# A fused attention-and-mixer kernel: the order of TensorE written out as a table of steps

## The chip, the cores and the metric

One core of a Trainium2 chip runs the program. The metric is the device time of one execution in microseconds (us); the kernel before was timed three times, and one further execution was recorded by the hardware profiler. Engine names are those of the profile: PE is TensorE (PEld its weight loads), DVE is VectorE, ACT is ScalarE, POOL is GpSimd, SP is SyncE, which here only issues DMAs. A name with a q (POOLq, SPq) is an engine's queue of issued DMAs.

## The reference

There are 8 batches with 8 heads, 512 tokens of 64 values each, and a state of 32 rows per head. Tokens read from the state, the state reads from the tokens, and the 544 rows that come out are mixed per batch.

```python
# attention, x: [8, 8, 512, 64], state: [8, 8, 32, 64]
scores = scale * x @ state.T           # softmax over the 32 state rows
xread  = softmax(scores) @ state
scores2 = scale * state @ x.T          # softmax over the 512 tokens
sread  = softmax(scores2) @ x
x = concat([xread, sread])             # [8, 544, 512] with the heads joined
# mixer, w_q and w_k: [512, 64], w_out: [512, 512]
wq, wk = x @ w_q, x @ w_k
W_tok  = scale2 * wq @ wk.T            # [544, 544] per batch
out    = relu(W_tok @ x) @ w_out       # [8, 544, 512]
```

Neither kernel builds `xread` or `W_tok`. Both use that the products are associative: `wq` is taken as (softmax) times (state times `w_q`), and `W_tok @ x` as `wq` times (`wk.T @ x`).

## The kernel before, in words

All of x, 8 MiB in float32, is brought in at the start. Batch 0 arrives as float32 in four pieces (`x_f0`, L71, issued from ACT) and is cast to bf16 by DVE and ACT (L427, L429). The other seven batches (`x_bf1` to `x_bf7`, L88 and L90) and `w_out` (L92, between batches 2 and 3) are cast by their DMA, which POOL issues. The state (`st_f`, L69 and L72) and `w_q`, `w_k` (`w_f`, L76) come through SP.

One batch goes through these steps, each with a matmul group on PE and, for most, an instruction on DVE, ACT or POOL that takes the result out of PSUM:

- `s_xT`: 16 transposes of x (L147), two copies by DVE (L152).
- `s_pt`: 16 matmuls for the scores (L161), Exp by ACT into `E` (L169), a sum per row and its reciprocal by DVE (L174, L176), the normalised `A` by POOL (L178).
- `s_stbd`: POOL spreads the state into a block diagonal, two instructions (L190).
- `s_at`: 8 transposes of `A` (L203), one copy (`AT`, L207).
- `s_srd`: 32 matmuls for the state's read and 8 for its sums (L216, L226), then `srn` by DVE (L235, L237) and the block diagonal `sbd` by POOL (L242). `s_srT`: one transpose of `srn` (L253), one copy (L255).
- `s_wqk`: 4 and 8 matmuls for `wq` (L264, L273), 8 and 16 for `wk` (L285, L294), one copy each (L281 ACT, L302 DVE). `s_g` (L310, L318) and `s_v` (L326, L330, L338) make `V`, the product of `wk` and the rows.
- `s_mix` (L348): two groups of four matmuls, each with a Relu, one on ACT (L357) and one on DVE (L359); `s_mix_s` (L367, L374) is the same for the 32 state rows, kept in `rmix_s`.
- `s_fin_mm`: 16 matmuls with `w_out` (L382), two copies by ACT (L393), each followed by a DMA of 512 KB to HBM from SP (L397). The last batch is copied and stored by quarters (L403, L406). After every fourth batch `s_fin_s` does the state rows of four batches together (L412, L420).

The loop runs over ten rounds. Round i starts batch X = i (`s_xT`, `s_pt`, `s_srd`), takes batch Y = i − 1 through `s_at` to `s_v`, and finishes batch Z = i − 2. The program is written with a tile framework: the program text gives dependencies and a priority, and a list scheduler places the instructions of all five engines at compile time, each engine then running its own in that fixed order. Tiles of a pool share a number of buffers, and an instruction that writes a tile waits until the buffer's former reader is done. PSUM has eight banks: pool `psA` holds three tiles of two banks (xT, scores, mix, fin, and sw of the start), pool `psB` two tiles of one bank (all the others).

At the start `setup_st` transposes the state (L103) and copies it into `stT` (L111, L113), and `setup_sw` multiplies it with the two weights (L124, copies L135, L137).

## Time and profile before

| what | value |
|---|---|
| device time, median of 3 runs | 116.53 us (115.98 to 117.35) |
| the profiled execution's own time | 116.32 us |
| its span, first to last instruction | 114.5 us |
| PE busy | 87.3 us, 76% |
| PE weight loads busy | 54.8 us, 48% |
| DVE busy | 58.2 us, 51% |
| ACT busy | 47.3 us, 41% |
| POOL busy | 43.3 us, 38% |
| HBM read, written | 10.22 MB, 8.91 MB |

The page gives busy times for the whole span, and slices of 2.86 us below them. The busy time of PE is modelled for overlapping matmuls, so the distance from one start to the next is the better measure of what a group of matmuls costs. The page's row of the granted TensorE clock rests on records that begin only some 26 us into the span. In the timeline a row begins with its start and its duration in us; in brackets stands how long the engine had been idle, and what ended that.

### The profile page before, as it was taken

The numbers are of one execution on the slowest core, as the hardware profiler recorded it, in microseconds if no ns is written. First come the engines' busy times: TensorE is split into PE (matmuls) and PEld (weight loads), VectorE is DVE, ScalarE is ACT, GpSimd is POOL, SyncE is SP. The second block draws the span as 40 slices with busy tenths as digits, with TensorE's granted clock in tenths as the row PEclk, the third lists the DMA queues.
The fourth block names the chain that finished last, engine by engine and source line by source line (L and its number), as shares of the span: only waits on it lengthen the run. The fifth ranks groups of instructions, "written<-read, shape, count | busy, mean of one in ns | idle before, by whom it ended". The sixth has DMA issues, their size and how long they took to land. (4 is left out here: it accounts for less than half of the span.)

```text
span 114.5 us, 3055 instructions
## 1 busy us (share of the span) xinstructions
PE 87.3 (76%) x1321; PEld 54.8 (48%) x1336; DVE 58.2 (51%) x117; ACT 47.3 (41%) x70; POOL 43.3 (38%) x55
## 2 busy tenths in 40 slices
PE   0223398684979999999999989989998997949600
PEld 0002375684655657366555726565674554524200
DVE  1325565658423727852953694296449435344200
ACT  0522449030163346438442644544573454480210
POOL 8995000583990390086058107700630640000000
PEclk9999999999755999999999999999999999999995
DMA  1999999999900044040404404052332224044381
GB/s 39 290 287 183 197 204 197 199 197 198 126 0 0 6 183 182 7 186 6 183 0 189 180 3 167 24 192 77 157 154 74 104 84 183 0 203 187 87 298 48
DMA packets 14933, 15.13 MB, mean 132 GB/s; under 512 B 3656, under 2 KB 12360, under 8 KB 14920
## 3 DMA queue, kind: packets, MB, share of 16 engines
q0 software_dynamic: 7808, 4.19, 26.3%
q1 hardware_dynamic: 5736, 9.18, 22.5%
q10 hardware_dynamic: 1376, 1.57, 4.6%
q8 instruction: 10, 0.16, 0.6%
q14 instruction: 3, 0.02, 0.1%
HBM read 10.22 MB, written 8.91 MB: 167 GB/s over the span
## 5 line engine op out<-in xcount | busy, mean ns | idle before, releaser
L382 PE MATMUL fin_ps<-w_o,rmix 128*128 128x512 bf16 x113 | 32.7, 386 | 4.9 <-ACT rmix L357 2.2
L178 POOL TENSOR_TENSOR A<-E,rinv 128x1024 bf16<-128x1024 bf16 x8 | 15.3, 1912 | 47.3 <-DVE rinv L176 28.8
L393 ACT COPY ost<-fin_ps 128x1024 f32<-128x1024 f32 x14 | 14.2, 1012 | 10.8 <-PE fin_ps L382 10.4
L147 PE MATMUL xT_ps<-ident,x_bf 128*128 128x128 bf16 x128 | 13.0, 252 | 6.1 <-ACT x_bf L429 3.0
L382 PEld LDWEIGHTS <-rmix 128*128 128x128 bf16 x128 | 10.7, 99 | 14.4 <-issue 2.8
L152 DVE COPY xT<-xT_ps 128x1024 bf16<-128x1024 bf16 x16 | 11.0, 686 | 12.4 <-PE xT_ps L147 12.4
L147 PEld LDWEIGHTS <-x_bf 128*128 128x128 bf16 x128 | 9.7, 112 | 9.3 <-ACT x_bf L429 3.5
L169 ACT ACTIVATE E<-pt_ps 128x1024 bf16<-128x1024 f32 x8 | 8.2, 1023 | 11.9 <-PE pt_ps L161 11.9
L359 DVE TENSOR_SCALAR rmix<-mix_ps 128x1024 bf16<-128x1024 f32 x8 | 9.7, 1218 | 6.5 <-PE mix_ps L348 6.5
L174 DVE TENSOR_REDUCE rsum<-E 128x32 f32<-128x1024 bf16 x8 | 9.7, 1213 | 2.8 <-ACT E L169 2.8
L338 ACT ACTIVATE V<-v_ps 128x512 bf16<-128x512 f32 x8 | 4.8, 597 | 14.9 <-PE v_ps L330 14.9
L242 POOL TENSOR_TENSOR sbd<-srn,mask 128x256 bf16<-128x256 bf16 x16 | 9.5, 612 | 1.8 <-DVE srn L237 1.7
L190 POOL TENSOR_TENSOR stbd<-st_bf,mask 128x256 bf16<-128x256 bf16 x16 | 9.4, 611 | 0.0
L357 ACT ACTIVATE rmix<-mix_ps 128x1024 bf16<-128x1024 f32 x8 | 8.2, 1028 | 1.3 <-PE mix_ps L348 1.3
L103 PE MATMUL stT_ps<-ident,st_bf 128*128 128x128 bf16 x16 | 2.6, 305 | 6.9 <-DVE st_bf L96 4.0
L302 DVE CAST wk<-wk_ps 128x384 bf16<-128x384 f32 x8 | 4.4, 548 | 6.6 <-PE wk_ps L294 6.6
L348 PE MATMUL mix_ps<-wq,V 64*128 64x256 bf16 x64 | 6.7, 291 | 1.2 <-ACT V L338 0.7
L161 PE MATMUL pt_ps<-stT,xT 128*128 128x64 bf16 x128 | 6.9, 212 | 0.0
L203 PE MATMUL at_ps<-ident,A 128*128 128x128 bf16 x64 | 6.5, 244 | 0.0
L161 PEld LDWEIGHTS <-xT 128*128 128x128 bf16 x128 | 6.2, 112 | 0.4
L281 ACT CAST wq<-wq_ps 128x288 bf16<-128x288 f32 x8 | 3.2, 402 | 6.5 <-PE wq_ps L273 6.5
L90 POOL DMA_DIRECT2D x_bf<-in_x_dram x6 | 5.6, 958 | 0.0
(64 smaller groups left out, 110.1 us busy)
## 6 DMA issues: line engine op xcount, KB each, us to landing
out_dram<-ost SPq DMA_DIRECT2D x14, 512.0 KB, 2.6
x_bf<-in_x_dram POOLq DMA_DIRECT2D x7, 512.0 KB, 17.6
x_f<-in_x_dram ACTq DMA_DIRECT2D x4, 256.0 KB, 5.8
w_o<-in_moe_w_out_dram POOLq DMA_DIRECT2D x1, 512.0 KB, 13.0
out_dram<-ost_s SPq DMA_DIRECT2D x2, 256.0 KB
out_dram<-ost SPq DMA_DIRECT2D x2, 256.0 KB, 3.6
out_dram<-ost ACTq DMA_DIRECT2D x2, 256.0 KB, 4.9
st_f<-in_state_dram SPq DMA_DIRECT2D x1, 448.0 KB
```

The lines of the kernel that those rows point to most:

```text
L147: nc.tensor.transpose(out=ps[:, u, h, :], in_=x_bf[b][:, h, 128 * u : 128 * u + 128], identity=ident,)
L152: nc.vector.tensor_copy(out=xT[:, u], in_=ps[:, u])
L161: nc.tensor.matmul(out=ps[:, 2 * u : 2 * u + 2, r, NS * q : NS * q + NS], lhsT=L["xT"][:, u, h, :], rhs=stT[:, b, h, :, :], start=(h == 0) ...
L169: nc.scalar.activation(out=E.rearrange("p c r q n -> p c r (q n)"), in_=ps, func=AF.Exp, scale=float(scale))
L174: nc.vector.reduce_sum(out=rsum, in_=Ev, axis=AX.X)
L178: nc.gpsimd.tensor_tensor(out=A.rearrange("p c r q n -> p (c r q) n"), in0=Ev, in1=rinv[:, :, None].to_broadcast((128, NC * 2 * NP, NS)), ...
L190: nc.gpsimd.tensor_tensor(out=stbd[:, r], in0=st_bf[:, b, r, 0:1, :].to_broadcast((128, NP, D)), in1=mask[:, :, None].to_broadcast((128, N ...
L242: nc.gpsimd.tensor_tensor(out=sbd[:, r], in0=srn[:, r : r + 1, :].to_broadcast((128, NP, D)), in1=mask[:, :, None].to_broadcast((128, NP, D)),
L357: nc.scalar.activation(out=dst, in_=ps, func=AF.Relu)
L359: nc.vector.tensor_scalar(out=dst, in0=ps, scalar1=0.0, scalar2=None, op0=ALU.max)
L382: nc.tensor.matmul(out=L["fin"][:, c % 2, :], lhsT=rmix[:, b, k, c // 2, 128 * (c % 2) : 128 * (c % 2) + 128], rhs=w_o[:, k, :], start=(k ...
L393: nc.scalar.copy(out=L["ost"], in_=L["fin"])
```

## The change: what it does

All steps are rewritten as small functions, one for each matmul group and one for each instruction that empties it, and a table `ORDER` lists them in the order in which they are recorded. An entry is step, batch and engine: `xT1.5.t` is the second half of the transposes of batch 5 on PE, `xTe1.5.a` its copy, on ACT. `manual_schedule` for PE alone keeps PE's instructions in the order of the table; those of DVE, ACT, POOL and SP are still placed by the list scheduler, with the table's order as priority. In the table the batches run 0, 1, 2, 3, then 5, 6, 4 and 7 overlapped, and an entry ends in `1` where a matmul group of the last batch writes a one-bank tile.

What else is different:

- PSUM: `psA` holds two tiles of two banks (mix, fin, sw), `psB` four tiles of one bank. xT and the scores are split into halves of one bank, and with them the Exp (16 of 512 elements a row instead of 8 of 1024) and the row sums. Work tiles have four buffers instead of three.
- Which engine empties a tile is chosen entry by entry: ten of the 16 copies of xT, three of the 8 of `AT`, five of the 8 of `wk` go to ACT, six of the 14 copies of `ost` to DVE; of the 16 Relus over `mix` 12 are on ACT.
- Loads: of the four pieces of `x_f0` two are issued from SP, ahead of the rest of the state, and two from ACT. POOL casts one of them (`xc0`) before it issues any load of x, and casts `w_f` (`wc`) between the issues of batches 3 and 4. The issue of batch 7 stands behind the first `sbd`.
- The block diagonal of the state, `stbd`, is no longer made by POOL for each batch. POOL clears a tile for all batches, and four DMAs from SP copy `st_bf` into its diagonal blocks.
- The state's transposes are 32 of 64 columns instead of 16 of 128. The matmuls of L294 become 8 per batch instead of 16, since `srT` is stored twice side by side. Over the whole program PE has 48 matmuls and 48 weight loads less.

On POOL, the start of the program before (x_bf_74 to x_bf_80 are batches 1 to 7, stT the state's transpose) reads:

```order
masks.py:197 MEMSET ident 128x128
L79 MEMSET stT 128x1792
masks.py:199 ISA
masks.py:199 AFFINE_SELECT ident<-ident 128x128
L88 DMA x_bf_74<-in_x_dram 128x8x256
L90 DMA x_bf_75<-in_x_dram 128x8x256
L92 DMA w_o<-in_moe_w_out_dram 128x4x512
L90 DMA x_bf_76<-in_x_dram 128x8x256
L90 DMA x_bf_77<-in_x_dram 128x8x256
L90 DMA x_bf_78<-in_x_dram 128x8x256
L90 DMA x_bf_79<-in_x_dram 128x8x256
L90 DMA x_bf_80<-in_x_dram 128x8x256
```

The same engine from its clearing of `stbd` on, after the change (x_bf_69 is batch 0, x_bf_70 to x_bf_76 are batches 1 to 7, x_f_77 the float32 tile of batch 0):

```order
L124 MEMSET stbd 128x2048
masks.py:199 ISA
masks.py:199 AFFINE_SELECT ident<-ident 128x128
L152 CAST x_bf_69<-x_f_77 128x512
L146 DMA x_bf_70<-in_x_dram 128x8x256
L146 DMA x_bf_71<-in_x_dram 128x8x256
L143 DMA w_o<-in_moe_w_out_dram 128x4x512
L146 DMA x_bf_72<-in_x_dram 128x8x256
L157 CAST w_qk<-w_f 128x4x128
L158 CAST w_qk<-w_f 128x4x64
L146 DMA x_bf_73<-in_x_dram 128x8x256
L146 DMA x_bf_74<-in_x_dram 128x8x256
```

Every load of x now stands behind a cast that waits for a piece of batch 0, and those of batch 4 and later behind casts that wait for the weights.

On ACT, one full round of the program before, in the middle of the run:

```order
L169 ACTIVATE E<-pt_ps 128x1024
L393 COPY ost<-fin_ps 128x1024
L281 CAST wq<-wq_ps 128x288
L338 ACTIVATE V<-v_ps 128x512
L393 COPY ost<-fin_ps 128x1024
L357 ACTIVATE rmix<-mix_ps 128x2x2x256
L374 ACTIVATE rmix_s<-mixs_ps 128x4x32
```

And ACT after the change, from the second Relu pair on (xT_919 and xT_912 are halves of batches 6 and 5, AT, ost and G as before):

```order
L137 ACTIVATE rmix<-mix_ps 128x2x2x256 x2
L131 COPY xT_919<-xT_ps 128x1024
L131 CAST wk<-wk_ps 128x384
L131 COPY xT_912<-xT_ps 128x1024
L457 ACTIVATE V<-v_ps 128x512
L253 ACTIVATE E<-pt_ps 128x512
L137 ACTIVATE rmix_s<-mixs_ps 128x4x32
L137 ACTIVATE rmix<-mix_ps 128x2x2x256 x2
L131 COPY ost<-fin_ps 128x1024
L131 COPY srT<-srT_ps 128x256
```

The regular round is gone: copies of xT and of `wk` and both Relus of a batch now stand between the Exps on ACT.

The diff, cut to its core:

```diff
+ORDER = """
+stc.0.v stt.0.t xc0.0.p ste.0.v stf.0.a xc1.0.a ix1.0.p xc2.0.v ix2.0.p xc3.0.v xT0.0.t iwo.0.p
...
+rinv.2.v pt0.3.t srTe.2.a xT1.5.t wke.0.v exp0.3.a A.2.p xT1.4.t swe.3.v g.0.t xTe1.5.a srd.3.t
...
+    ctx.enter_context(tc.manual_schedule(engines={mybir.EngineType.PE}))
...
-    work = ctx.enter_context(tc.tile_pool(name="work", bufs=3))
-    ostp = ctx.enter_context(tc.tile_pool(name="ostp", bufs=3))
-    psA = ctx.enter_context(tc.tile_pool(name="psA", bufs=3, space=bass.MemoryType.PSUM))
-    psB = ctx.enter_context(tc.tile_pool(name="psB", bufs=2, space=bass.MemoryType.PSUM))
+    work = ctx.enter_context(tc.tile_pool(name="work", bufs=4))
+    psA = ctx.enter_context(tc.tile_pool(name="psA", bufs=2, space=bass.MemoryType.PSUM))
+    psB = ctx.enter_context(tc.tile_pool(name="psB", bufs=4, space=bass.MemoryType.PSUM))
...
-        nc.scalar.dma_start(out=x_f0[:, 2 * g : 2 * g + 2], in_=xsrc(0, 2 * g, 2 * g + 2))
+        eng = nc.sync if g % 2 == 0 else nc.scalar
+        eng.dma_start(out=x_f0[:, 2 * g : 2 * g + 2], in_=xsrc(0, 2 * g, 2 * g + 2))
...
-    nc.gpsimd.memset(stT[:, 1:B].bitcast(FP), 0.0)
-    nc.vector.memset(stT[:, 0].bitcast(FP), 0.0)
+    nc.vector.memset(stT.bitcast(FP), 0.0)
+    nc.gpsimd.memset(stbd.bitcast(FP), 0.0)
...
+    def load_x(n, b, e):
+        if n == "iwo":
+            nc.gpsimd.dma_start(out=w_o, in_=moe_w_out.rearrange("(k p) e -> p k e", p=128))
+        else:
+            b = int(n[2:])
+            nc.gpsimd.dma_start(out=x_bf[b], in_=xsrc(b, 0, H))
...
+    def w_cast(n, b, e):
+        nc.gpsimd.tensor_copy(out=w_qk[:, :, 0:2, :], in_=w_f)
+        nc.gpsimd.tensor_copy(out=w_qk[:, :, 2, :], in_=w_f[:, :, 1, :])
...
+    def st_cast(n, g, e):
+        b0, b1 = (0, 1) if g == 0 else (1, B)
+        copy(e, st_bf[:, b0:b1], st_f[:, b0:b1])
+        if g == 1:
+            for q in range(NP):
+                rows = slice(NS * q, NS * q + NS)
+                nc.sync.dma_start(
+                    out=stbd[rows, :, :, q, :].rearrange("p b r d -> p (b r) d"),
+                    in_=st_bf[rows].rearrange("p b r d -> p (b r) d"),
+                )
...
+    def xT_mm(n, b, e):
+        u = int(n[-1])
+        ps = psB.tile([128, H, 128], BF, name="xT_ps", tag="psB")
...
+    def xT_ev(n, b, e):
+        u = int(n[-1])
+        xT = work.tile([128, H, 128], BF, name=f"xT{u}")
+        copy(e, xT, L[b][f"xT{u}"])
...
+    def pt_mm(n, b, e):
+        u = int(n[-1])
+        ps = psB.tile([128, 2, 2, HN], FP, name="pt_ps", tag="psB")
...
+    def wks_mm(n, b, e):
+        ps = psB.tile([128, NC + 2, DH], FP, name="wk_ps", tag="psB")
+        for q in range(NP):
+            for h in range(2):
+                nc.tensor.matmul(
+                    out=ps[64 * h : 64 * h + 64, NC : NC + 2, :],
+                    lhsT=L[b]["srT"][:, q, :, :],
...
+    def fin_mm(n, b, e):
+        c = int(n[-1])
+        if e == "1":
+            ps = psB.tile([128, DM], FP, name="fin1_ps", tag="psB")
+            L[b][n] = ps
...
+    for tok in ORDER.split():
+        n, b, e = tok.split(".")
+        STEP[n.rstrip("0123456789")](n, int(b), e)
```

## The prediction

> **What bounds the kernel now.** I read the page first, then its table by stretches, then PE's timeline in a late round, and last the loads. Of the page:

> ```profile
> PE 87.3 (76%) x1321; PEld 54.8 (48%) x1336; DVE 58.2 (51%) x117; ACT 47.3 (41%) x70; POOL 43.3 (38%) x55
> ...
> PEclk9999999999755999999999999999999999999995
> DMA  1999999999900044040404404052332224044381
> ```

> No engine is full over the span, and the 16 DMA engines are full until slice 11, some 31 us. So I cut the span at the ends of rounds; the columns after the stretch are busy us and instructions of PE, PEld, DVE, ACT, POOL, then granted clock, DMA share, GB/s.

> ```profile
> 0.00:14.00 14.00, 2.97 (x20) 1.75 (x21) 5.25 (x19) 3.99 (x7) 9.59 (x15) 1.00 1.06 199
> 14.00:27.00 13.00, 11.12 (x192) 9.12 (x190) 8.38 (x17) 5.15 (x10) 4.19 (x5) 1.00 1.41 199
> 27.00:42.28 15.28, 12.98 (x225) 8.27 (x227) 7.43 (x17) 5.22 (x8) 9.77 (x13) 0.78 0.40 73
> ...
> 52.37:62.54 10.17, 9.54 (x155) 5.78 (x156) 6.04 (x11) 5.04 (x8) 4.23 (x6) 1.00 0.27 106
> ...
> 40.00:90.00 50.00, 47.25 (x725) 28.86 (x736) 30.20 (x55) 25.56 (x36) 19.59 (x24) 1.00 0.29 113
> ```

> From 40 us on PE is the bound: 47.25 of 50 busy, ACT 25.56 (0.51), DVE 30.20 (0.60). Before that it is not, and what it does there it does slowly:

> ```profile
> 13.81 1.06 PE L147 MATMUL xT_ps<-ident,x_bf 128*128 128x128 bf16 x8
> ...
> 28.22 0.41 PE L264 MATMUL wq_ps<-AT,sw 128*64 128x256 bf16 x4 [1.50 <-DVE AT L207]
> ...
> 33.55 1.04 PE L203 MATMUL at_ps<-ident,A 128*128 128x128 bf16 x8
> ```

> Eight transposes take 1.06 us here and 0.61 in the late round below. The page's clock of 9 in the first slices has no record behind it; by these durations PE ran at half clock at 14 us, and again at 33.5, where the page has its 7 and 5. One round of the steady part:

> ```profile
> 52.37 0.61 PE L147 MATMUL xT_ps<-ident,x_bf 128*128 128x128 bf16 x8
> 52.91 0.39 PE L348 MATMUL mix_ps<-wq,V 64*128 64x256 bf16 x4
> ...
> 53.32 0.23 PE L203 MATMUL at_ps<-ident,A 128*128 128x128 bf16 x1
> 53.68 0.29 PE L348 MATMUL mix_ps<-wq,V 64*128 64x256 bf16 x2
> ...
> 55.06 0.65 PE L161 MATMUL pt_ps<-stT,xT 128*128 128x64 bf16 x16
> 55.55 0.38 PE L382 MATMUL fin_ps<-w_o,rmix 128*128 128x512 bf16 x1
> 55.98 0.22 PE L253 MATMUL srT_ps<-ident,srn 128*128 128x128 bf16 x1
> 56.43 0.82 PE L382 MATMUL fin_ps<-w_o,rmix 128*128 128x512 bf16 x3 [0.23 <-DVE rmix L359]
> 57.18 0.41 PE L264 MATMUL wq_ps<-AT,sw 128*64 128x256 bf16 x4
> 57.52 1.25 PE L382 MATMUL fin_ps<-w_o,rmix 128*128 128x512 bf16 x5
> 58.71 0.30 PE L273 MATMUL wq_ps<-srT,w_qk 128*64 128x32 bf16 x8
> 58.94 0.41 PE L285 MATMUL wk_ps<-sw,AT 128*128 128x64 bf16 x8
> 59.28 0.41 PE L294 MATMUL wk_ps<-w_qk,srT 128*32 128x128 bf16 x16
> 59.79 0.42 PE L216 MATMUL srd_ps<-x_bf,E 128*32 128x64 bf16 x32
> 60.15 0.35 PE L226 MATMUL srd_ps<-ones,E 128*128 128x1 bf16 x8
> 60.36 0.39 PE L310 MATMUL g_ps<-wk,A 128*128 128x64 bf16 x8
> 60.81 0.38 PE L382 MATMUL fin_ps<-w_o,rmix 128*128 128x512 bf16 x1
> 61.25 0.38 PE L326 MATMUL v_ps<-sbd,wk 128*128 128x512 bf16 x1
> ...
> 61.90 0.81 PE L382 MATMUL fin_ps<-w_o,rmix 128*128 128x512 bf16 x3
> 62.54 0.22 PE L147 MATMUL xT_ps<-ident,x_bf 128*128 128x128 bf16 x1
> ```

> Read from start to start: three matmuls of L382 take 62.54 − 61.90 = 0.64, 0.21 each. A single one at 55.55 takes 0.43, so 0.22 is lost, and 0.23 more at 60.81. The one transpose at 55.98 takes 0.45 where a transpose costs 0.54/8 = 0.07: 0.38 lost. At 53.32 it is 0.36 − 0.07, at 60.36 0.45 against 0.21 for as many matmuls at 60.15, at 59.28 0.51 against 0.34 at 58.94. Together 0.22 + 0.23 + 0.38 + 0.29 + 0.24 + 0.17 = 1.5. A round of 10.17 us thus holds about 8.7 us of matmuls, and waits are 17% on top of the work.

> **What the work is.** Eight batches of 8.7 are 69.6. The state rows at the end of four batches are two groups of four L382-like matmuls, 8 × 0.21 = 1.7. The state's 32 transposes at up to 0.07 and 64 small products with the weights at up to 0.03 (eight of L273 take 0.23) are at most 4.2; I take 2.6, and as they come early little hangs on it. That is 73.9 us at full clock, against 108.7 at which the last matmul ends. The 35 us between are idle at the start, half clock and waits. The change takes hold of this, not of the work: half the matmuls of L294 would save at most 0.17 a batch, but those left load twice as many columns, and 0.34 may stay 0.34. I take 0.05 a batch, 0.4 in all: 73.5.

> **The start.** How early PE can be kept full depends on the loads.

> ```profile
> L90 POOL DMA_DIRECT2D x_bf<-in_x_dram x6: 879/908/1108, 3.8 to 9.1; - x6
> L427 DVE CAST x_bf<-x_f x2: 478/602/726, 4.2 to 7.8; 128x512 bf16<-128x512 f32 x2
> ...
> L88 POOL DMA_DIRECT2D x_bf<-in_x_dram x1: 1060/1060/1060, 2.7 to 2.7; - x1
> ...
> DMA to landing us min/median/max: 9.8/17.6/22.6
> ```

> Batch 1 landed at 2.7 + 9.8 = 12.5, batch 7 at 9.1 + 22.6 = 31.7; between them seven loads, 2.75 each. In the table the first step that could starve PE late is `xT1.5`, which needs batch 5: before, 12.5 + 5 × 2.75 = 26.3. Two things push it back. The first load is issued behind a cast on POOL that waits for a piece of batch 0 (the first DVE cast of such a piece began at 4.2). A POOL cast of 512 elements has no row; DVE's row has 0.6, so issue moves from 2.7 to about 5, while landing was held by shared DMA engines: between 0 and 2.3 later. The four DMAs of `stbd` add 4 × 32 × 16 = 2048 packets of 128 bytes, in a time in which DMA engines are full:

> ```profile
> q1 hardware_dynamic: 3101, 0.77, 41.9%
> ```

> This is SP's queue between 2 and 12 us, nearly all packets of 256 bytes: 41.9% of 16 engines over 10 us is 67 us, 21.6 ns a packet, so 2048 cost 2.8 us if none is cheaper, and 0 if they fit into gaps. [...] That batches 4 to 7 wait on POOL behind the weights' casts costs nothing while four loads of 2.75 are queued ahead; batch 7's issue, behind `sbd` and so behind batch 1's landing, has till past 20 us. The stores behind `stbd` on SP come after 35 us. So batch 5 is there between 26.3 and 31.4; I take the middle, 29. By then the table has put 12.4 us of work on PE: 2.6 for state and weights, four batches of xT and scores (4 × (1.08 + 0.49) = 6.3), three of the state's read (3 × 0.57 = 1.7), and 1.8 of batch 0's `AT`, `wq`, `wk` and transposes. From batch 0's casts at about 7 that fits into 22 us even at half clock. What is left after `xT1.5` begins is 73.5 − 12.4 = 61.1, and with no wait at all it ends at 29 + 61.1 = 90.1.

> **The middle.** The 17% of waits have two sources in the rows above: a group waits for its tile to be emptied, and one batch's chain of `AT`, `wq`, `wk`, `g`, `v` has little between its links. The table puts groups of other batches there: between `pt0.4` and `at.4` stand three groups of L382, 2.6 us, and the sums and weights of others. Against it stands that DVE and ACT get more to do:

> ```profile
> L393 ACT COPY ost<-fin_ps 128x1024 f32<-128x1024 f32 x14 | 14.2, 1012 | 10.8 <-PE fin_ps L382 10.4
> L152 DVE COPY xT<-xT_ps 128x1024 bf16<-128x1024 bf16 x16 | 11.0, 686 | 12.4 <-PE xT_ps L147 12.4
> L190 POOL TENSOR_TENSOR stbd<-st_bf,mask 128x256 bf16<-128x256 bf16 x16 | 9.4, 611 | 0.0
> L338 ACT ACTIVATE V<-v_ps 128x512 bf16<-128x512 f32 x8 | 4.8, 597 | 14.9 <-PE v_ps L330 14.9
> ```

> After the change ACT has 33 instructions of 1024 elements (10 xT, 3 `AT`, 12 Relus, 8 `ost`) at 1.01, some 28 of 512 (16 Exps among them) at 0.60, and about 20 smaller ones at an estimated 0.45: 33 + 17 + 9 = 59 us, 12 more than 47.3. DVE gives ten copies of 0.69 away and takes six of `ost`; I leave it at 58. Of ACT's 59 about three quarters, 45, come after `xT1.5`. POOL loses the 9.4 us of L190, and was not waited for. So I take half of the 17%: 61.1 × 0.085 = 5.2, bounds 0 and 10.4. That PE keeps ACT busy for 45 of 66 us, 0.68, is more than its 0.51, and is the assumption I trust least.

> **The clock.** The row at 28.22 shows a wait of 1.50, and after it the page has slices of 7 and 5, about 6.8 us at half clock (0.78 over 15.28 us is a loss of 3.4). [...] So a wait for batch 5 can cost one such stretch: 0 to 3.4, and I take 1.

> **The end.** The last copy here is

> ```profile
> 108.76 0.59 ACT L406 COPY ost<-fin_ps 128x512 f32<-128x512 f32 x1 [2.14 <-PE fin_ps L382]
> ```

> right behind the last matmul, and the span ends at 114.5, 5.8 later, for one copy and one store. The change ends in the same two, so 5.8 stays; it has one-bank tiles for the last four groups, which at most saves a wait inside the work. The profiled execution took 116.32, 1.8 more than its span, and stands 0.2 below the median of 116.53.

> Sum: 90.1 + 5.2 + 1 + 5.8 + 1.8 = 103.9. Lowest, with batch 5 at 26.3 and waits of 2: 97. Highest, with 31.4, 10.4 and 3.4: 113.9.

> **Rivals.**

> 1. PE is nearly dense: batch 5 at 26.3, waits 0 to 3. For it: between the links of one batch's chain the table has other batches' groups almost everywhere. Against: in a strict order any one late tile stops all of PE. 26.3 + 61.1 + 7.6 and waits of 0 to 4: 95 to 99.
> 2. Late loads and a second fall of the clock: POOL's casts hold the queue and PE stalls on batches 5 to 7, at half clock after. 31.4 + 61.1 + 3.4 + 7.6 and waits of 4 to 10.4: 107 to 114.
> 3. ACT becomes the bound and PE's fixed order feeds it badly: each ACT instruction waits for a PE group that cannot be moved ahead of a waiting one, and PE waits for ACT. If ACT stays at its present share of 0.51 after 29 us, its 45 us take 88: 29 + 88 + 7.6 = 124.6, slower. It decides at a share of 45/(116.5 − 7.6 − 29) = 0.56; below that the change loses. For it: ACT's 12 us more, Relus and xT copies now in one queue with the Exps. Against: ACT's 0.51 was set by PE's own pace, with DVE reaching 0.60 beside it.
> 4. The gain at the start is handed back in the middle in equal parts, by a mean share of 0.55 to 0.57: no change.

> **How the numbers follow.** The forecast, 99 to 107, has 0.48; rival 1 0.13; rival 2 0.18; ACT as the bound, but still 114 to 115.3, 0.04; rival 4 0.06; rival 3 0.11. About 1% is what a measurement of this kernel can tell from no change. Faster: 0.48 + 0.13 + 0.18 + 0.04 = 0.83; same 0.06; slower 0.11. The range of 97 to 114 leaves out half of rival 1, rivals 3 and 4 and a little of the rest, about 0.2 with the 0.04.

> **What would show it.** In the profile after: batch 5's landing between 26 and 31; no transposes of 1.06 after some 30 us, else the clock; ACT's share above 0.6 and PE's busy share about 0.95 between 35 and 85 us; the last matmul near 96. An ACT share near 0.5 with PE idle before its groups "<-ACT" would show rival 3. I would be wrong altogether if PE's waits in the middle rise above 17%.

## The result and the profile after

The changed kernel takes 99.99 us (median of four runs, 99.42 to 100.5) where the kernel before took 116.33 beside it: a ratio of 0.858, interval 0.851 to 0.865. The profiled execution took 100.5 us, its span 98.7. The forecast was 103.9 with a range of 97 to 114.

From the page of the changed kernel: busy times, the slices for PE, its granted clock and the DMA engines, the instruction queue, and the shares of the chain that ended last.

```profile
PE 80.1 (81%) x1288; PEld 53.0 (54%) x1288; DVE 53.3 (54%) x107; ACT 56.9 (58%) x84; POOL 35.0 (35%) x42
...
PE   0137699654999999999999979999999999999200
...
PEclk9999999996559999999999999999999999999965
DMA  1999999999999200270324650283003255293980
...
q8 instruction: 10, 0.16, 0.7%
...
PE 60%; DMA 26%; POOL 3%; DVE 3%; ACT 2%; issue 1%; SPq 0%; ACTq 0%
```

The DMA engines are full until some 32 us, as before. The clock still has its dip, but in slices that begin at 22 us instead of 29 (a slice is 2.47 us here and was 2.86). From the eleventh slice on PE is full, with one exception, until the end. ACT took on 9.6 us. The stretches of the changed kernel (busy us and instructions of PE, PEld, DVE, ACT and POOL, then clock, DMA share and GB/s):

```profile
14.00:22.00 8.00, 6.00 (x188) 4.84 (x186) 6.65 (x16) 5.84 (x9) 6.95 (x10) 1.00 1.63 213
22.00:29.00 7.00, 5.70 (x121) 4.76 (x119) 3.20 (x7) 2.90 (x5) 4.25 (x4) 0.55 1.47 199
...
35.00:85.00 50.00, 49.16 (x733) 30.28 (x730) 29.45 (x55) 33.43 (x49) 12.30 (x13) 1.00 0.31 122
```

Between 35 and 85 us PE is busy 49.16 of 50, ACT 33.43, a share of 0.67. What stopped PE before that is in the timeline:

```profile
5.30 0.61 POOL L152 CAST x_bf<-x_f 128x512 bf16<-128x512 f32 x1 [2.29 <-DMA x_f<-in_x_dram]
...
11.78 0.62 ACT L253 ACTIVATE E<-pt_ps 128x512 bf16<-128x512 f32 x1
...
19.75 0.29 PE L321 MATMUL srd_ps<-ones,E 128*128 128x1 bf16 x6 [0.63 <-issue]
21.76 0.40 PE L295 MATMUL at_ps<-ident,A 128*128 128x128 bf16 x4 [0.90 <-POOL A L282]
23.69 1.89 PE L221 MATMUL xT_ps<-ident,x_bf 128*128 128x128 bf16 x16 [1.30 <-DMA x_bf<-in_x_dram]
...
29.41 1.14 PE L221 MATMUL xT_ps<-ident,x_bf 128*128 128x128 bf16 x16
```

The row at 23.69 is batch 3, whose load landed at 23.65 by the chain (issued at 8.53, 15.12 us under way, the largest part of DMA's 26%). Batch 5 landed at 29.08, and its transposes began at 29.41, the last row. From 29.4 us on, the list of PE's waits has a single entry (us in total, times, longest):

```profile
PE fins_ps L505 <- DVE rmix_s L139: 0.7, 1, 0.7
```

The timeline at the end:

```profile
86.63 5.35 PE L505 MATMUL fin_ps<-w_o,rmix 128*128 128x512 bf16 x24
...
93.31 0.58 ACT L131 COPY ost<-fin_ps 128x512 f32<-128x512 f32 x1 [2.42 <-DMA out_dram<-ost]
```

PE ends at 92.0, and 6.7 us follow. The last copy waits 2.42 us for the store that holds its buffer, 1.3 of them after its matmuls are done.

What the prediction had not seen is in the start of the kernel before. Its timeline on ACT and DVE:

```profile
12.37 0.62 ACT L116 CAST w_qk<-w_f 128x512 bf16<-128x512 f32 x1 [2.73 <-DMA w_f<-in_moe_w_k_dram]
12.40 0.29 DVE L117 CAST w_qk<-w_f 128x256 bf16<-128x256 f32 x1 [2.15 <-DMA w_f<-in_moe_w_k_dram]
12.81 0.67 DVE L152 COPY xT<-xT_ps 128x1024 bf16<-128x1024 bf16 x1
...
17.40 1.02 ACT L169 ACTIVATE E<-pt_ps 128x1024 bf16<-128x1024 f32 x1 [0.63 <-PE pt_ps L161]
```

Two casts of the mixer's weights stand at the head of both queues and wait for a load. The copies of batch 0 are queued behind them, and its Exp comes at 17.40; in the changed kernel, where POOL casts the weights, the first Exp is at 11.78.

### The profile page after: what moved, and what is told of

Read it like the earlier page. It is cut to its first block, busy times and chain, and to the rows that moved or that the text cites. A ratio compares the mean times of both kernels' runs of the same rounds, so it can differ in the third digit from the quotient of the medians.

```text
span 98.7 us, 2953 instructions
## 1 busy us (share of the span) xinstructions
PE 80.1 (81%) x1288; PEld 53.0 (54%) x1288; DVE 53.3 (54%) x107; ACT 56.9 (58%) x84; POOL 35.0 (35%) x42
## 3 DMA queue, kind: packets, MB, share of 16 engines
q0 software_dynamic: 7808, 4.19, 31.0%
## 4 chain that ended last, share of the span: by engine, by line
PE 60%; DMA 26%; POOL 3%; DVE 3%; ACT 2%; issue 1%; SPq 0%; ACTq 0%
PE fin_ps L505 22%; DMA x_bf<-in_x_dram 15%; DMA out_dram<-ost 6%; PE xT_ps L221 5%; PE mix_ps L471 4%; DMA x_f<-in_x_dram 4%; PE at_ps L295 3%; PE pt_ps L237 3%; PE wq_ps L371 3%; PE wk_ps L409 3%; PE srd_ps L308 2%; PE wk_ps L397 2%; PE fins_ps L505 2%; PE g_ps L425 2%; POOL x_bf L146 2%; PE v_ps L440 2%
## 5 line engine op out<-in xcount | busy, mean ns | idle before, releaser
L505 PE MATMUL fin_ps<-w_o,rmix 128*128 128x512 bf16 x128 | 29.9, 379 | 0.0
L282 POOL TENSOR_TENSOR A<-E,rinv 128x1024 bf16<-128x1024 bf16 (+1 forms) x8 | 14.4, 1804 | 21.4 <-DVE rinv L276 11.9
L131 ACT COPY ost<-fin_ps 128x1024 f32<-128x1024 f32 (+1 forms) x10 | 9.3, 927 | 10.1 <-PE fin_ps L505 6.1
L137 ACT ACTIVATE rmix<-mix_ps 128x1024 bf16<-128x1024 f32 x12 | 12.2, 1025 | 4.0 <-PE mix_ps L471 4.0
L133 DVE COPY ost<-fin_ps 128x1024 f32<-128x1024 f32 (+1 forms) x8 | 8.7, 1090 | 10.1 <-PE fin_ps L505 10.1
L268 DVE TENSOR_REDUCE rsum<-E 128x16 f32<-128x512 bf16 x16 | 10.7, 680 | 5.8 <-ACT E L253 5.7
L253 ACT ACTIVATE E<-pt_ps 128x512 bf16<-128x512 f32 x16 | 9.4, 604 | 4.3 <-PE pt_ps L237 3.8
L131 ACT COPY xT<-xT_ps 128x1024 bf16<-128x1024 bf16 x10 | 10.1, 1032 | 1.1 <-PE xT_ps L221 1.1
L133 DVE COPY xT<-xT_ps 128x1024 bf16<-128x1024 bf16 x6 | 4.1, 688 | 3.7 <-PE xT_ps L221 3.7
L139 DVE TENSOR_SCALAR rmix<-mix_ps 128x1024 bf16<-128x1024 f32 x4 | 4.9, 1220 | 0.8 <-PE mix_ps L471 0.8
L295 PEld LDWEIGHTS <-A 128*128 128x128 bf16 x64 | 3.9, 98 | 1.5 <-POOL A L282 1.0
## 6 DMA issues: line engine op xcount, KB each, us to landing
w_o<-in_moe_w_out_dram POOLq DMA_DIRECT2D x1, 512.0 KB, 12.8
```

Of the source, the lines that this page charges most:

```text
L131: nc.scalar.copy(out=out, in_=in_)
L133: nc.vector.tensor_copy(out=out, in_=in_)
L137: nc.scalar.activation(out=out, in_=in_, func=AF.Relu)
L253: nc.scalar.activation(out=L[b]["E"][:, 2 * u : 2 * u + 2].rearrange("p c r q n -> p c r (q n)"), in_=L[b][f"pt{u}"], func=AF.Exp, scale=f ...
L268: nc.vector.reduce_sum(out=L[b]["rsum"][:, w], in_=L[b]["E"].rearrange("p c r q n -> p (c r q) n")[:, w], axis=AX.X,)
L282: eng.tensor_tensor(out=L[b]["A"].rearrange("p c r q n -> p (c r q) n")[:, w], in0=L[b]["E"].rearrange("p c r q n -> p (c r q) n")[:, w], ...
```

## The experiments

Ratios are taken against runs of the kernel before on the same chip (medians 116.4 to 117.3). Where a time is worked out from a ratio, it is the ratio times 116.5.

**The binding order on PE alone.** The table stays, as a priority only.

```diff
-    ctx.enter_context(tc.manual_schedule(engines={mybir.EngineType.PE}))
```

> The changed kernel with PE, too, left to the list scheduler; the table stays as the priority. If the gain lies in the order of the batches that the table gives and not in its being binding, PE stays about 0.97 busy between 35 and 85 us and the time is 99 to 102. If the binding order is what keeps PE fed, the list scheduler's own choices bring back waits of the size of the old rounds (17% of about 60 us): 105 to 111.

100.72 us, ratio 0.862 (0.854 to 0.869), not to be told from the changed kernel. PE is busy 48.71 of 50 between 35 and 85 us. Binding the order on PE is worth nothing here that can be measured; the priorities do the work.

**The new parts in the old rounds.** All new steps, tiles, loads and the table's choice of engines, but the entries sorted into the rounds of the kernel before, placed by the list scheduler on all engines. A piece of the table, batch 4 starting:

```diff
-    ctx.enter_context(tc.manual_schedule(engines={mybir.EngineType.PE}))
...
+sbd.3.p g.2.t ge.2.v fin2.1.t v.2.t ve.2.a fin3.1.t oe1.1.a xT0.4.t xTe0.4.a xT1.4.t xTe1.4.v
+mix0.2.t mxe0.2.a mix1.2.t mxe1.2.v mixs.2.t mse.2.a at.3.t ate.3.v pt0.4.t exp0.4.a pt1.4.t
```

> The changed kernel's steps, tiles, loads and choice of engines, but the table written in the old rounds (batch i begins, i-1 in the middle, i-2 finishes) and all engines placed by the list scheduler, as before. Theory, that the order across batches is the gain: PE starves again between 14 and 35 us and waits of about 1 us a batch come back, 110 to 115. Rival, that one-bank tiles, the loads and the new sharing of copies are the gain: 101 to 104.

106.41 us, ratio 0.910 (0.904 to 0.916): between the two, so the order matters, but more than half of the gain is there without it. What PE waits for between 35 and 85 us in this run (us in total, times, longest):

```profile
PE fin_ps L505 <- ACT rmix L137: 2.0, 4, 0.7
PE fin_ps L505 <- DVE rmix L139: 0.7, 1, 0.7
PE pt_ps L237 <- ACT xT L131: 0.7, 2, 0.5
...
```

**The weights' casts alone.** The kernel before, with the two casts on POOL and recorded first.

```diff
-        nc.scalar.copy(out=w_qk[:, :, 0:2, :], in_=w_f)
-        nc.vector.tensor_copy(out=w_qk[:, :, 2, :], in_=w_f[:, :, 1, :])
+        nc.gpsimd.tensor_copy(out=w_qk[:, :, 0:2, :], in_=w_f)
+        nc.gpsimd.tensor_copy(out=w_qk[:, :, 2, :], in_=w_f[:, :, 1, :])
...
+    setup_w()
     for i in range(B + 2):
...
-            setup_w()
```

> The kernel before, with only the two casts of the mixer's weights moved from ACT and DVE to POOL, behind its load issues. In the trace before, DVE and ACT sat idle until 12.4 us before these casts, with the copies of batch 0's xT and state queued behind them. Theory, that this one wait set the start: the copies of xT run from about 10 us, batch 0's Exp comes at 13 instead of 17.4, and the time falls by 3 to 5 us, to 112 to 114. Rival, that the loads of x and the old order set the start anyway: within 1 us of the kernel before.

109.23 us, ratio 0.934 (0.929 to 0.940), more than expected: the place of two instructions of 0.3 and 0.6 us cost 7.6 us. Its timeline:

```profile
10.55 0.67 DVE L152 COPY xT<-xT_ps 128x1024 bf16<-128x1024 bf16 x1
12.45 0.61 POOL L116 CAST w_qk<-w_f 128x512 bf16<-128x512 f32 x1 [2.44 <-DMA w_f<-in_moe_w_k_dram]
...
14.11 1.02 ACT L169 ACTIVATE E<-pt_ps 128x1024 bf16<-128x1024 f32 x1
```

The same wait now stands on POOL, where nothing urgent is behind it. The first copy of xT comes 2.26 us earlier, the Exp 3.3. The stretch of 6.8 us at half clock (0.50 from 29.9 to 36.7 before), worth 3.4, is gone too: the recorded clock is 1.00 until the work ends. Wait and clock together would be 6.7 of the 7.6. The first matmul with `w_out` starts at 28.8 us instead of 35.3, so 6.5 of the gain lie ahead of it, and a steady round stays as long as it was (10.18 us against 10.17).

**The casts put back into the changed kernel**, at the same place of the table.

```diff
-        nc.gpsimd.tensor_copy(out=w_qk[:, :, 0:2, :], in_=w_f)
-        nc.gpsimd.tensor_copy(out=w_qk[:, :, 2, :], in_=w_f[:, :, 1, :])
+        nc.scalar.copy(out=w_qk[:, :, 0:2, :], in_=w_f)
+        nc.vector.tensor_copy(out=w_qk[:, :, 2, :], in_=w_f[:, :, 1, :])
```

> The changed kernel with one thing undone: the two casts of w_f go back to ACT and DVE, at the same place in the table. They wait for w_f, which lands near 12 to 15 us, and on ACT the copies of stT and xT of batch 0 are queued behind. Theory, that this wait at the head of a queue was a large part of the gain: the first Exp moves from 11.8 to 15 to 17 us, and the time rises by 3 to 6, to 103 to 106. Rival, that in this order the landing of batch 3 near 23.7 sets the pace whatever stands ahead of it: PE still starts batch 3 within 0.5 us of 23.7, and the time rises by 1 at most, to 100 to 101.

104.33 us, ratio 0.893 (0.886 to 0.900): 4.1 us slower, as the theory has it. ACT in this run:

```profile
14.70 0.62 ACT L157 CAST w_qk<-w_f 128x512 bf16<-128x512 f32 x1 [9.70 <-DMA w_f<-in_moe_w_k_dram]
15.34 0.37 ACT L131 COPY stT<-stT_ps 64x256 bf16<-64x256 bf16 x1
15.73 1.93 ACT L131 COPY xT<-xT_ps 128x1024 bf16<-128x1024 bf16 x2
17.55 0.62 ACT L253 ACTIVATE E<-pt_ps 128x512 bf16<-128x512 f32 x1
```

Batch 3's transposes on PE start late:

```profile
27.09 1.06 PE L221 MATMUL xT_ps<-ident,x_bf 128*128 128x128 bf16 x16
```

Their load had landed at 22.08: here PE's own late start sets the pace, not the load.

**The PSUM tiles alone**, on top of the kernel with POOL's casts.

```diff
-    psA = ctx.enter_context(tc.tile_pool(name="psA", bufs=3, space=bass.MemoryType.PSUM))
-    psB = ctx.enter_context(tc.tile_pool(name="psB", bufs=2, space=bass.MemoryType.PSUM))
+    psA = ctx.enter_context(tc.tile_pool(name="psA", bufs=2, space=bass.MemoryType.PSUM))
+    psB = ctx.enter_context(tc.tile_pool(name="psB", bufs=4, space=bass.MemoryType.PSUM))
...
-        ps = psA.tile([128, NC // 2, H, 128], BF, name="xT_ps", tag="psA")
...
+            ps = psB.tile([128, H, 128], BF, name="xT_ps", tag="psB")
...
+            ps = psB.tile([128, 2, 2, HN], FP, name="pt_ps", tag="psB")
```

> The kernel before with its two casts of w_f on POOL took 109.2; with the new tiles, loads, stbd and engine choices as well, and with its old order of rounds, the program took 106.4. This run adds only the tiles to the first: psA two tiles of two banks, psB four of one bank, xT, scores and Exp in halves. Theory: the tiles explain most of those 2.8 us: 106.0 to 107.5. Rival: the tiles buy nothing here, since a round's chain waits for its own copies and not for a free tile, and the 2.8 us came from the loads and the choice of engines: 108.5 to 110.

102.6 us, ratio 0.879 (0.873 to 0.885). Both sums were wrong: the tiles are worth 6.5 us, more than the whole 2.8 that was to be split. A piece of one round with the old tiles (the run with POOL's casts alone):

```profile
46.76 0.62 PE L147 MATMUL xT_ps<-ident,x_bf 128*128 128x128 bf16 x8
...
48.41 0.59 PE L382 MATMUL fin_ps<-w_o,rmix 128*128 128x512 bf16 x2
48.84 0.22 PE L253 MATMUL srT_ps<-ident,srn 128*128 128x128 bf16 x1
49.30 0.82 PE L382 MATMUL fin_ps<-w_o,rmix 128*128 128x512 bf16 x3 [0.24 <-DVE rmix L359]
...
56.94 0.62 PE L147 MATMUL xT_ps<-ident,x_bf 128*128 128x128 bf16 x8
```

And with the new ones:

```profile
44.94 0.63 PE L162 MATMUL pt_ps<-stT,xT 128*128 128x64 bf16 x16
45.41 1.10 PE L385 MATMUL fin_ps<-w_o,rmix 128*128 128x512 bf16 x4
46.35 0.22 PE L256 MATMUL srT_ps<-ident,srn 128*128 128x128 bf16 x1
46.50 0.41 PE L267 MATMUL wq_ps<-AT,sw 128*64 128x256 bf16 x4
...
53.90 0.63 PE L162 MATMUL pt_ps<-stT,xT 128*128 128x64 bf16 x16
```

A round takes 56.94 − 46.76 = 10.18 us with the old tiles and 53.90 − 44.94 = 8.96 with the new, in the same rounds and with the same engines; only where the list scheduler puts PE's groups within a round differs, too. The lone transpose holds PE for 0.46 us there and for 0.15 here, and the groups of four matmuls with `w_out` are no longer cut up. From the first of these matmuls for batch 0 to the first for batch 7 the traces have 67.2 us (28.8 to 96.0) and 62.0 (27.6 to 89.6): 5.2 of the 6.5 us, the rest is ahead of them. PE's busy time hardly shows it (47.66 of 50 between 35 and 85 us against 48.87): the waits lie between groups that the profile counts as overlapping. Two things come with this cut, more tiles of one bank and the work in halves, and no run separates them here. Nor does the longest stall in the old round's rows name a tile: the 0.46 us at 48.84 end with a Relu's result (the row at 49.30).

This left the program with the new parts in old rounds 3.6 us behind a kernel that has only two of these parts. Its loads or its choice of engines had to cost that.

**The old choice of engines in the same rounds.** Forty-eight entries of the run of 106.4 change their last letter; one line of its table:

```diff
-xTe1.2.a mix0.0.t mxe0.0.a mix1.0.t mxe1.0.a mixs.0.t mse.0.v at.1.t ate.1.v pt0.2.t exp0.2.a
+xTe1.2.v mix0.0.t mxe0.0.a mix1.0.t mxe1.0.v mixs.0.t mse.0.a at.1.t ate.1.v pt0.2.t exp0.2.a
```

> The rounds of the kernel before, as in the run that took 106.4, with only the choice of engines in the rounds put back: all copies of xT and AT on DVE, one Relu of a batch on ACT and one on DVE, the wide copies of ost, wq, V and rmix_s on ACT, srT, wk and G on DVE. The kernel before with POOL's casts and the new tiles took 102.6. Theory: the 3.8 us between these two are the engine choice, which fits the table's order and not the rounds: PE busy in 35 to 85 us rises from 45.3 to above 48, and the time is 102 to 104. Rival: they are the new loads and the DMAs for stbd: PE stays below 46.5, and the time is 105 to 107.

102.26 us, ratio 0.876 (0.870 to 0.882). The stretch of 35 to 85 us, with the table's engines in rounds, and then with the old ones:

```profile
35.00:85.00 50.00, 45.33 (x737) 28.92 (x746) 30.34 (x60) 31.39 (x47) 15.35 (x15) 1.00 0.30 117
```

```profile
35.00:85.00 50.00, 49.41 (x778) 29.86 (x775) 32.02 (x64) 27.53 (x44) 15.49 (x15) 1.00 0.31 121
```

PE gains 4.1 us in this stretch alone. The longest waits listed above for the run of 106.4 are for ACT's Relus (2.0 us), and in that stretch they are absent here. A likely reading is that with both Relus of a batch one behind the other on ACT, the rounds make PE wait for the second, where the table's order has other batches' work; as 48 entries change at once, that is argued and not shown. The loads, the DMAs for `stbd` and the other new steps, which this run has and the one of 102.6 has not, come out together at no difference.

**One PSUM tile less.** Three one-bank tiles in the changed kernel.

```diff
-    psB = ctx.enter_context(tc.tile_pool(name="psB", bufs=4, space=bass.MemoryType.PSUM))
+    psB = ctx.enter_context(tc.tile_pool(name="psB", bufs=3, space=bass.MemoryType.PSUM))
```

> The changed kernel with three one-bank PSUM tiles instead of four. Theory, that the order across batches leaves PE almost no wait for a tile: PE's busy share between 35 and 85 us falls from 0.98 to 0.95 at most, the time by under 2 us more: 100 to 102. Rival, that the fourth tile is what keeps PE fed: waits of the old size, 17% of 60 us, 105 to 110.

104.46 us, ratio 0.895 (0.889 to 0.901), 4.3 us slower and between the two expectations. PE falls to 47.27 of 50 between 35 and 85 us. The fourth tile, too, is a large part of what keeps PE dense.

**ACT made heavier.** Six copies of `ost` and four Relus move from DVE to ACT, some 10 us.

```diff
-oe1.0.v
+oe1.0.a
...
-mxe1.2.v
+mxe1.2.a
...
-mxe0.6.v
+mxe0.6.a
```

> The changed kernel with the six copies of ost and the four Relus that stand on DVE moved to ACT: 10 us more for ACT, whose share between 35 and 85 us would go from 0.67 to 0.85. Theory, that PE is the bound and ACT has room: at most 2 us slower, 100 to 102. Rival, that a fixed order on PE makes ACT the bound well below full: 105 or more, with PE idle ahead of groups that ACT releases.

101.47 us, ratio 0.868 (0.862 to 0.875). ACT is busy 40.33 of 50 between 35 and 85 us, a share of 0.81, and PE still 48.72. At 0.67 ACT is not the bound. The 10 us on ACT cost some 1.2 us in all (the intervals touch), and PE now waits for ACT's Relus, 0.30 to 0.71 us at a time.

**`stbd` by POOL instead of by DMA**, two instructions a batch as in the kernel before.

```diff
-        if g == 1:
-            for q in range(NP):
...
-                nc.sync.dma_start(
...
+    def st_bd(n, b, e):
+        for r in range(2):
+            nc.gpsimd.tensor_tensor(
```

> The state's block diagonal made by POOL again, two instructions a batch, in place of the four DMAs of 2048 packets. Theory, that these packets held up the loads by 2.8 us: batch 3 lands near 21 and batch 5 near 26.3, and as PE is waiting for batch 3 in the changed kernel, the time falls to 97 to 99. Rival, that POOL's 9.4 us come back as later A and the clock's low stretch eats the rest: 99.5 to 102.

102.49 us, ratio 0.873 (0.864 to 0.881). The loads do come earlier (batch 5 at 27.39 instead of 29.08), so the 2048 small packets cost some 1.7 us of loading (in two more runs with the same loads as the changed kernel, the binding order dropped and the last copies' own buffer, batch 5 lands at 28.9 and 28.7). But the list scheduler put ten of these instructions on POOL ahead of the `A` that PE needs:

```profile
25.41 5.74 POOL L348 TENSOR_TENSOR stbd<-st_bf,mask 128x256 bf16<-128x256 bf16 x10
31.12 1.90 POOL L276 TENSOR_TENSOR A<-E,rinv 128x1024 bf16<-128x1024 bf16 x1
```

PE waits for it, and the clock falls there (half from 34.3 to 37.8 us):

```profile
33.08 0.62 PE L289 MATMUL at_ps<-ident,A 128*128 128x128 bf16 x8 [2.81 <-POOL A L276]
```

In the changed kernel PE waits for POOL's `A` once, for 0.90 us (the row at 21.76 above). What the DMAs cost or save where POOL is free isn't shown by this run.

**The load of `w_out` behind that of batch 5.** In the table:

```diff
-xT0.0.t iwo.0.p xT1.0.t
+xT0.0.t xT1.0.t
...
-ix5.0.p xTe1.1.a
+ix5.0.p iwo.0.p xTe1.1.a
```

> The load of w_out is issued behind batch 5 instead of ahead of batch 3, nothing else. Batches 3, 4 and 5 land 2.7 us earlier (21, 23.7, 26.4), and PE's wait for batch 3 goes. Theory, that from there on the landing of batch 5 binds: last matmul 2.5 earlier, 97 to 98. Rival, that PE at half clock from 22.7 to 29.6 us is the bound there, so that earlier data find it still busy: at most 1.3 earlier, 98.7 to 100.

99.78 us, ratio 0.854 (0.849 to 0.860): no difference. Batch 5 landed 2.7 us earlier, and its transposes began at 27.68 instead of 29.41, but PE waited 0.92 and 1.14 us with no releaser in the trace (the last section has more of this kind) and 0.95 for POOL's `A`, and the last matmul ended at 91.64 instead of 92.0. The earlier load bared the next waits at once.

**A buffer of its own for the last copies.**

```diff
-        ost = work.tile([128, DM], FP, name="ost1")
+        ost = work.tile([128, DM], FP, name="ost2")
```

> The changed kernel with a pool of its own for the four quarters of the last batch's output, so that the last copy no longer waits for the store of the state rows. In the changed kernel's trace that copy sat 2.4 us, 1.3 of them after its matmuls were done. Theory: 1.3 us less, ratio to the changed kernel 0.987. Rival, that the stores queued before it end the run anyway: no difference, within 0.4 us.

100.13 us, ratio 0.857 (0.853 to 0.862): no difference. In this run the last copy starts right behind its matmuls:

```profile
91.99 0.59 ACT L131 COPY ost<-fin_ps 128x512 f32<-128x512 f32 x1 [1.14 <-PE fin_ps L505]
92.61 0.36 ACTq L531 DMA_DIRECT2D out_dram<-ost  x1
```

It is 1.3 us earlier than in the changed kernel, and its store landed at 97.11 where the other landed at 97.01. What ends last is the queue of stores: in the changed kernel five of them land between 94.5 and 97.0.

**Four edits together.** From the two before, and the two waits of PE that a move in the table can take away.

```diff
-xT0.0.t iwo.0.p xT1.0.t
+xT0.0.t xT1.0.t
...
-ix5.0.p xTe1.1.a
+ix5.0.p iwo.0.p xTe1.1.a
...
-rs0.1.v ix7.0.p at0.0.t
+rs0.1.v at0.0.t
...
-A1.0.p pt1.2.t
+A1.0.p ix7.0.p pt1.2.t
...
-mxe1.3.v fs.3.t xTe0.4.a
+mxe1.3.v xTe0.4.a
...
-fin0.3.t fse.3.v
+fin0.3.t fs.3.t fse.3.v
...
-        ost = work.tile([128, DM], FP, name="ost1")
+        ost = work.tile([128, DM], FP, name="ost2")
```

> The changed kernel with four small edits: the load of w_out is issued behind that of batch 5, the load of batch 7 behind both parts of A of batch 1, the state rows' last product behind the first of batch 3's, and the last copies have a buffer of their own. Theory: batch 5 lands near 26.4 instead of 29.1, the wait of 0.9 for A of batch 1 and that of 0.73 for the state rows' Relu go, the last matmul ends near 90.5 instead of 92.0: 98.0 to 99.3. Rival: the freed time is eaten at the start by waits for instructions and at the end by the stores: 99.4 to 100.3, no difference.

98.87 us, ratio 0.848 (0.844 to 0.852), about 1.2% under the changed kernel, the two intervals touching. The fastest of all, as the theory has it: batch 5 landed at 25.84, the last matmul ended at 90.2. But waits of the kind that the rival names are in it too. PE's waits now:

```profile
19.76 0.29 PE L321 MATMUL srd_ps<-ones,E 128*128 128x1 bf16 x6 [0.76 <-issue]
...
25.96 0.30 PE L201 MATMUL sw_ps<-w_qk,stT 64*32 64x128 bf16 x15 [1.18 <-issue]
31.97 0.40 PE L295 MATMUL at_ps<-ident,A 128*128 128x128 bf16 x4 [1.30 <-issue]
```

Together 3.2 us of waits that neither data nor a buffer explains.

The path from the kernel before to the changed one, by ratios:

| kernel | ratio | us | step |
|---|---|---|---|
| before | 1 | 116.5 | |
| weights' casts on POOL | 0.934 | 108.9 | −7.6 |
| and one-bank tiles, xT, scores and Exp in halves | 0.879 | 102.4 | −6.5 |
| and new steps and loads, `stbd` by DMA, same rounds and engines | 0.876 | 102.1 | none |
| and the table's engines, still in rounds | 0.910 | 106.0 | +3.9 |
| and the table's order as a priority | 0.862 | 100.4 | −5.6 |
| and that order binding on PE: the changed kernel | 0.858 | 100.0 | none |

The steps hold for this sequence: the casts, 7.6 us in the kernel before, are 4.1 in the changed one.

## Why the prediction was right, and where not

The time lay in the range, 3.9 us under the forecast. In the profiled execution, 3.4 under it, the middle is 4.7 less than forecast, the end 0.9 more and the start of `xT1.5` 0.4 later. By the steps of its sum:

- **Batch 5's landing, 29: right.** It landed at 29.08, and its transposes began at 29.41. The first load's issue did move from 2.75 to 5.86, but its data landed at 12.8 instead of 12.5, nearly the lower end of the 0 to 2.3; `stbd`'s packets cost most of the 2.8. That PE's own work would be there in time held: the transposes began 0.33 us after the data. The reason given for it does not come out, as 12.4 us of work are 24.8 at half clock and not the 22 that were there. Other runs show that this was luck in part: with the casts back, PE was 5 us behind the loads, and with the loads 2.7 us earlier nothing was gained. The load that did stop PE was batch 3's, which the prediction never looked at, since it began its sum at batch 5.
- **The work, 61.1: right as far as the trace tells.** From 29.41 to the last matmul's end at 92.0 are 62.6 us, waits included.
- **The waits in the middle, 5.2 for half of 17%: the term that was mis-sized.** With the 1 us for the clock, 6.2 were put on top of the 61.1, and 1.5 are left, 0.73 of them one wait for the Relu of the state rows. The reason taken, the table's filling of gaps, is the smaller part of it: order and engines together brought 2.1 us on top of rounds with the new tiles. Most of the waits between the links of one batch's chain go with the new cut of PSUM: with four one-bank tiles and the work in halves, a round in its old order already takes 8.96 us, 3% over the 8.7 of work that the prediction had counted. With three such tiles, in the table's order, 4.3 us come back. The prediction gave the tile as one of two sources and then priced both with the table.
- **ACT, 0.68: right,** at 0.67. Rival 3, ACT as the bound with a threshold of 0.56, falls: at 0.81 PE is still full.
- **The clock, 1 us after batch 5's landing.** It was half from 22.8 to 29.6, so nearly all of it came ahead of that landing, in time that the loads set anyway.
- **The end, 5.8: it is 6.7.** A free buffer did not shorten it; that the 0.9 is the queue of stores is read from their landings.
- **POOL "was not waited for":** true of the kernel before, but not of the changed one, where PE waits 0.90 us for POOL's `A`, 0.95 in the run with `w_out` later and 2.81 in the run with `stbd` on POOL.

Of the rivals, the first (a dense PE) had the middle right and the landing at 26.3 wrong; the runs that brought the landing there came out at 98.9 and 99.8, at or just above the upper end of its 95 to 99. The second had a second fall of the clock, but it came ahead of batch 3 and not through batches 5 to 7, and no such waits followed. The fourth, no change, falls with the result. The chances that the prediction leaves outside its range add up to 0.28 (half of 0.13, 0.06, 0.11 and 0.04), where it says about 0.2.

The one thing the sum could not show, because it started at a landing, is what made the kernel before slow at the start: the casts at the head of two queues, 7.6 of the 16.5 us. The prediction had quoted DVE's copies of xT by their waits for PE, and did not look at what stood ahead of the first of them in DVE's queue.

## What to carry to other kernels

Before an order written by hand is credited with a gain, undo the small parts that came with it: here an instruction moved out of the head of a queue and a different cut of PSUM brought 14 of the 16.5 us with the old order in place. Read a steady round from start to start (a PE that was busy 95% of the time hid rounds that could be 12% shorter), and try the cut of PSUM by itself. A choice of engines belongs to an order: the one of the table cost 3.9 us in rounds and fitted its own.
